# Two groups' second layer in one pass, its first product by Strassen's seven block products

## The chip, the cores and the metric

The kernel runs on one core of a Trainium2 chip. The metric is device time in microseconds (us) of one launch, the median of several runs. Five engines work from queues of their own, each strictly in its order: PE (TensorE, matrix products), DVE (VectorE), ACT (ScalarE), POOL (GpSimd) and SP (SyncE, here only the issuer of transfers).

## The reference

Three stages follow each other on 1152 tokens (batch 2 x 576) of width 512. In short:

```python
# attention, 8 heads of 64, causal, with a bias from cumulated gates
cum = cumsum(maximum(s, 0), axis=-1)
scores = where(causal, -1e9, q @ k.T / 8 + minimum(-(cum[q] - cum[k]), 0))
x = softmax(scores) @ v                      # -> (1152, 512)
# layer 1: 512 -> 2048 -> 512, w_in and w_out
h = x @ w_in
x = where(h > 0, h, exp(minimum(h, 0)) - 1) @ w_out
# layer 2: E = 4 experts, 512 -> 1024 -> 512, weighted by p = probs / sum(probs)
for e in range(4):
    out += p[:, e:e+1] * (maximum(x @ w1[e], 0) @ w2[e])
```

## The kernel before

The tokens are cut into three groups, `GROUPS` = (0, 256), (256, 384), (640, 512) as (first token, tokens). For each group the kernel does attention, then layer 1, then layer 2. A layer's weights are cut into *units* of 128 hidden columns: a unit is one tile [128, 1024], its first half the piece of the first matrix (four blocks of 128 input rows), its second half the piece of the second. Layer 1 has `NAB` = 16 units, layer 2 has `E * NCD` = 4 x 8 = 32.

*Precision.* Except in layer 1 of the first group, an fp32 product is made of three matmuls of rounded operands (`three`, L540): high x high, high x low, low x high. So weights are split once for each group by `prepare` (L77): ACT rounds (L81), DVE takes the remainder (`split_lo`, L64).

*A unit.* `up1` or `up2` makes the hidden values of all the group's tokens, 4 x 3 matmuls with the tokens as columns, into a PSUM bank `up`; ACT and DVE apply the nonlinearity and split the result into `gt`. `LAG` = 2 units later `down1` (12 matmuls into four banks acc0 to acc3, result transposed) or `down2` (3 matmuls of 512 columns for each 128 tokens) adds the unit's share of the second product. In layer 2 the four accumulators run over the 8 units of an expert, then DVE scales them by p and adds them to `osb` (L710, L712); at the last expert the tile goes out (L715). Between the layers the accumulated `yacc` is rounded by ACT and split by DVE into yh and yl (L682).

*Transfers.* Layer 1's weights come coded (`w64`), 32 half units; the decoder borrows free tiles for them, and writes the decoded units to HBM (`w_dec`), from where the later groups load them. `fetch` (L72) loads units into `raw` (three buffers), `prepare` works from there.

*Order.* `slot` (L576) is the loop's step: `up` of a unit, preparation of later units (`advance`), `down` of an earlier one. Attention of the *next* group is cut into small parts (`attention_parts`) that `Background` hands out evenly between `BG_FROM` and `BG_TO`: the middle group's from slot 14 of the first group to its end, the last group's from slot 17 of the middle group (where its layer 2 begins) to its end. A scheduler then fixes each engine's order from this.

Of the kernel before, what the change touches and what calls it, by code (L numbers as in the profile page):

```python
# [25 lines left out]
GROUPS = [(0, 256), (256, 384), (640, 512)]  # L26
CHUNKS = [[0, 128, 256, 384, 512, 576], [0, 64, 192, 320, 448, 576]]
JOBS = [
    [],
    [(0, (2, 3, 4), 0), (1, (0,), 320)],  # L30
    [(1, (1, 2), 0), (1, (3, 4), 256)],
]

# [5 lines left out]
BG_FROM = [14, 17, 0]  # L39
BG_TO = [1, 2, 0]  # L40
# [7 lines left out]
def tile_kernel(ctx, tc, qT, kT, v, s, w64, w, probs, out):  # L48
    nc = tc.nc
    pool = ctx.enter_context(tc.tile_pool(name="sb", bufs=1))  # L50
    psum = ctx.enter_context(tc.tile_pool(name="ps", bufs=1, space=bass.MemoryType.PSUM))
    PE, DVE, ACT, POOL, SP = nc.tensor, nc.vector, nc.scalar, nc.gpsimd, nc.sync

    def sb(shape, tag, bufs, dtype=F32):
        return pool.tile(shape, dtype, tag=tag, name=tag, bufs=bufs)
# [13 lines left out]
    n_units = NU * len(GROUPS)  # L69
    fetched, units = {}, {}  # L70

    def fetch(n):  # L72
        u = n % NU
        fetched[n] = t = sb([128, 1024], "raw", 3)
        SP.dma_start(out=t, in_=w_dec[u] if u < NAB else w[u - NAB])
# [11 lines left out]
    small = [(t, 1, 1) for t in ("yh0", "yl0", "yh1", "yl1")] + [("raw", 3, 1)] * 3 + [("xl", 1, 2)]  # L87
    turn = [("wu", 5, 2)] * N_WU + [("gt", 3, 1)] * N_GT + small * 5
# [24 lines left out]
    def decode_halves(upto):  # L113
# [4 lines left out]
        while n_decoded[0] < min(upto, len(order)):  # L118
# [10 lines left out]
            z = sb([128, 512], f"osb{i % 2}", 1, I32)  # L129
# [198 lines left out]
    def attention_parts(g, xh, xl):  # L328


        items, jobs = [], ([], [])
        for b, chunks, col in JOBS[g]:
            cb = CHUNKS[b]
            q0, q1 = cb[chunks[0]], cb[chunks[-1] + 1]
            for hp in range(HP):
                job = dict(b=b, chunks=chunks, col=col, q0=q0, q1=q1, hp=hp, small=q1 == 64)
# [5 lines left out]
                jobs[job["small"]].append(job)  # L342

        def load_small():

            b = jobs[1][0]["b"]
            q, k, ck, vv = (sb([128, HP, 1, n], t + "s", 1)
                            for t, n in (("q2", 64), ("k2", 64), ("cbp", 64), ("v", 128)))
            for t, x in ((q, qT), (k, kT)):
                SP.dma_start(out=t[:, :, 0], in_=x[b, :, 0:64].rearrange("(c p) n -> p c n", p=128))  # L350
            for j in range(2):
                rows = cum_d[b * H:b * H + H, 0:64].rearrange("(o c j) k -> o j c k", o=1, j=2)
                SP.dma_start(out=ck[64 * j:64 * j + 64, :, 0],
                             in_=rows[:, j].to_broadcast([64, HP, 64]))
            SP.dma_start(out=vv[:64].rearrange("p c o n -> p (c o n)"), in_=v[b, 0:64])
            for job in jobs[1]:
                hp = job["hp"]
                job["q"], job["k"], job["cump"], job["v"] = q[:, hp], k[:, hp], ck[:, hp], vv[:, hp]
                job["pt"] = sb([128, 2, 1, 64], "pts", HP)

        def load(job):
# [30 lines left out]
            job["pt"] = buf([128, 2, nc_, nq], "pt")  # L392
# [22 lines left out]
        def qk(it, pss, a, e):  # L415
# [9 lines left out]
            for jj in range(2):  # L425
                r = slice(64 * jj, 64 * jj + 64)
                x = 0 if job["small"] else jj
                PE.matmul(pss[r, :e - a], job["q"][r, x, qs], job["k"][r, x, a:e],  # L428
# [37 lines left out]
        def transposes(it, cs):  # L466
# [5 lines left out]
            for m, c in enumerate(cs):  # L472
                PE.transpose(pt[:cb[c + 1] - cb[c], m, :], p[:, cb[c]:cb[c + 1]], ident)  # L473
            dst, m0 = job["pt"], 0
# [14 lines left out]
        def values(job):  # L489
# [11 lines left out]
            ACT.activation(xh[:, hp, xs], o[:, :nq], AF.Copy)  # L501
            split_lo(xl[:, hp, xs], o[:, :nq], xh[:, hp, xs])
            big = jobs[0]
            if job in big and big.index(job) + 2 < len(big):
                load(big[big.index(job) + 2])
# [4 lines left out]
        def start():  # L510
            with late():
                for job in jobs[0][:2]:
                    load(job)
                if jobs[1]:
                    load_small()
# [79 lines left out]

    x_first = sb([128, NCC, GROUPS[0][1]], "xh", 1)
    attention_first(x_first)
    cum_columns(0, 4)
    cum_columns(1, 0)
    n_use = 0  # L600
    x_parts = None
    for g, (t0, tok) in enumerate(GROUPS):
        n_tile = tok // 128
# [19 lines left out]
        class Lazy(list):  # L623

            def __init__(self, f, n):
                super().__init__([None] * n)
                self.f, self.got = f, None

            def __getitem__(self, i):
                if self.got is None:  # L630
                    self.got = self.f()
                return self.got[i]

        def up1(n, k, x):
# [141 lines left out]
```

## Time and profile before

| | us |
|---|---|
| median of 3 runs | 737.17 (736.9 to 739.24) |
| the profiled execution | 739.13 |
| its span, first to last instruction | 737.2 |
| PE busy | 707.3 (96%) |
| PE weight loads busy | 601.1 (82%) |
| DVE busy | 450.2 (61%) |
| ACT busy | 384.5 (52%) |

Stages on PE, by the chain: start and attention of the first group to 35.5 us; its layer 1 to 104.6 and layer 2 to 227.3; the middle group's layer 1 to 300.8 and layer 2 to 467.8; the last group's layer 1 to 558.9 and layer 2 to 731.2. A line number stands for a line of the kernel; L544 is the matmul in `three`, so all its products share it, and are told apart by their tiles and columns. Idle time of an engine counts only where it is the one that others wait for.

### The profile page before, as it was taken

The page shows a single profiled execution, that of the slowest core. Times are in us where ns is not written, and L with a number is a line of the kernel's source. Part 1 is how long each engine was busy: PE and PEld are TensorE (multiplying, and loading weights), DVE is VectorE, ACT ScalarE, POOL GpSimd, SP SyncE. Part 2 cuts the span into 40 slices and gives each one's busy share as a digit, 9 for nine tenths or more (in the row PEclk, how much of TensorE's full clock was granted, in tenths as well). Part 3 has the DMA queues.
Part 4 walks back from the last instruction along what each step waited for, and adds up shares of the span by engine and source line. Part 5 has one row for each costly group of instructions (what it writes and reads, how often), then busy time and mean ns, then how long its engine had stood idle before and what let it go on. Part 6 is the DMA issues. An engine that isn't in the chain of part 4 may idle for free.

```text
span 737.2 us, 10366 instructions
## 1 busy us (share of the span) xinstructions
PE 707.3 (96%) x3738; PEld 601.1 (82%) x3738; DVE 450.2 (61%) x899; ACT 384.5 (52%) x766; POOL 13.6 (2%) x33
## 2 busy tenths in 40 slices
PE   5489799999999999999999999999999999999997
PEld 4378678878879999888888888888888888888886
DVE  4678687977766666868777664565554344343432
ACT  4978676866645454766665555444344323332220
POOL 2001000000000000000000000000000000000000
PEclk9599999999999999999999999999999999999999
DMA  9689988755645343455543332333233232332301
GB/s 323 237 300 389 279 281 228 200 186 162 194 147 197 116 130 127 122 175 153 179 135 103 117 102 86 130 120 108 86 106 94 88 112 86 94 106 87 114 1 57
DMA packets 45298, 111.64 MB, mean 151 GB/s; under 512 B 7392, under 2 KB 18528, under 8 KB 45248
## 3 DMA queue, kind: packets, MB, share of 16 engines
q1 hardware_dynamic: 42784, 102.34, 43.7%
q0 software_dynamic: 2304, 8.39, 2.8%
q8 instruction: 29, 0.48, 0.3%
q10 hardware_dynamic: 160, 0.26, 0.1%
q14 instruction: 21, 0.17, 0.1%
HBM read 99.96 MB, written 11.01 MB: 151 GB/s over the span
## 4 chain that ended last, share of the span: by engine, by line
PE 83%; DVE 5%; DMA 5%; ACT 4%; issue 2%; SPq 0%; DVEq 0%; ACTq 0%
PE acc L544 37%; PE up L544 37%; PE att L498 3%; PE att L473 3%; DMA raw<-in_w 1%; ACT wu L128 1%; DVE wu L131 1%; PE att L422 1%; PE att L420 1%; DMA q<-in_qT 1%; ACT osb L130 1%; DMA wu<-in_w 1%; DMA yh<-in_w 1%; PE att L428 1%; PE up L640 1%
## 5 line engine op out<-in xcount | busy, mean ns | idle before, releaser
L544 PE MATMUL acc<-wu,gt 128*128 128x512 f32 x864 | 226.8, 398 | 0.0
L64 DVE TENSOR_TENSOR wu<-raw,wu 128x1024 fp32r<-128x1024 f32 x128 | 156.6, 1223 | 113.5 <-ACT wu L81 113.4
L544 PE MATMUL up<-yh,wu 128*128 128x256 f32 (+2 forms) x768 | 208.4, 340 | 0.0
L81 ACT ACTIVATE wu<-raw 128x1024 fp32r<-128x1024 f32 x128 | 135.5, 1059 | 94.3 <-PE acc L544 92.7
L544 PEld LDWEIGHTS acc<-wu,gt 128*128 128x128 f32 x864 | 155.7, 188 | 30.7 <-issue 3.2
L544 PEld LDWEIGHTS up<-yh,wu 128*128 128x128 f32 x768 | 136.6, 188 | 13.3 <-issue 1.2
L544 PE MATMUL up<-yl,wu 128*128 128x256 f32 (+2 forms) x384 | 129.3, 337 | 0.6 <-DVE yl L64 0.6
L726 ACT ACTIVATE gt<-up 128x256 fp32r<-128x256 f32 (+2 forms) x96 | 46.9, 489 | 93.8 <-PE up L544 93.4
L544 PE MATMUL acc<-gt,wu 128*128 128x384 f32 (+1 forms) x384 | 81.3, 362 | 0.0
L727 DVE SCALAR_TENSOR_TENSOR gt<-up,gt 128x256 fp32r<-128x256 f32 (+2 forms) x96 | 53.2, 554 | 44.5 <-ACT gt L726 44.2
L544 PEld LDWEIGHTS up<-yl,wu 128*128 128x128 f32 x384 | 72.4, 189 | 7.6 <-DVE yl L64 1.7
L544 PE MATMUL up<-xh,wu 128*128 128x384 f32 (+1 forms) x256 | 77.0, 362 | 0.0
L544 PEld LDWEIGHTS acc<-gt,wu 128*128 128x128 f32 x384 | 69.5, 188 | 7.5
L544 PEld LDWEIGHTS up<-xh,wu 128*128 128x128 f32 x256 | 47.4, 188 | 5.1
L644 ACT ACTIVATE e<-up 128x256 f32<-128x256 f32 (+2 forms) x48 | 23.4, 488 | 47.1 <-PE up L544 42.7
L544 PE MATMUL up<-xl,wu 128*128 128x384 f32 (+1 forms) x128 | 46.3, 362 | 0.0
L463 ACT ACTIVATE p<-p,nm 128x576 f32<-128x576 f32 (+6 forms) x56 | 34.5, 616 | 15.5 <-DVE nm L458 15.2
L640 PE MATMUL up<-xh,wu 128*128 128x256 f32 x128 | 32.0, 394 | 6.4 <-DVE gt L648 5.5
L655 ACT ACTIVATE gt<-e 128x384 fp32r<-128x384 f32 (+1 forms) x32 | 18.5, 577 | 32.8 <-DVE e L652 32.8
L458 DVE CUSTOM_DVE_ANT_0 p<-att,mask 128x384 f32<-128x384 f32 (+5 forms) x48 | 25.2, 525 | 15.5 <-PE att L422 15.5
L640 PEld LDWEIGHTS up<-xh,wu 128*128 128x128 f32 x128 | 24.7, 197 | 11.0 <-DVE gt L648 6.7
L473 PE MATMUL att<-ident,p 128*128 128x128 f32 (+1 forms) x192 | 32.1, 273 | 0.6 <-DVE p L438 0.3
(135 smaller groups left out, 673.5 us busy)
## 6 DMA issues: line engine op xcount, KB each, us to landing
raw<-in_w SPq DMA_DIRECT2D x105, 512.0 KB
raw<-w_dec SPq DMA_DIRECT2D x32, 512.0 KB
w_dec<-wu POOLq DMA_DIRECT2D x16, 512.0 KB, 7.0
k<-in_kT SPq DMA_DIRECT2D x16, 288.0 KB
yh<-in_w SPq DMA_DIRECT2D x6, 512.0 KB
yl<-in_w SPq DMA_DIRECT2D x6, 512.0 KB
xl<-in_w SPq DMA_DIRECT2D x6, 512.0 KB
out<-osb SPq DMA_DIRECT2D x9, 256.0 KB
```

Of the source, the lines that this page charges most:

```text
L64: DVE.tensor_tensor(out=lo, in0=x, in1=hi.bitcast(F32), op=ALU.subtract)
L81: ACT.activation(t[:, 0], x, AF.Copy)
L458: DVE.tensor_tensor_reduce(p[:, a:e], pss[:, :e - a], it["bias"][:, a:e], -1.0 / SC, it["low"], ALU.add, ALU.min, nm)
L463: ACT.activation(p, p, AF.Exp, bias=nm, scale=-1.0, accum_out=sm)
L473: PE.transpose(pt[:cb[c + 1] - cb[c], m, :], p[:, cb[c]:cb[c + 1]], ident)
L498: PE.matmul(o[64 * j:64 * j + 64, qs:nq], job["v"][:n, c, 64 * j:64 * j + 64], job["pt"][:n, j, c, qs:nq], start=c == 0, stop=c == n_c - 1)
L544: PE.matmul(o, a[m], b[n], start=first and i == 0, stop=last and i == 2)
L640: PE.matmul(o, t[:, dm(c)], x[:, c], start=c == 0, stop=c == NCC - 1)
L644: ACT.activation(e, o, AF.Exp)
L655: ACT.activation(gt[:, 0], e, AF.Copy)
L726: ACT.activation(ht[:, 0], o, AF.Relu)
L727: DVE.scalar_tensor_tensor(out=ht[:, 1], in0=o, scalar=0.0, in1=ht[:, 0].bitcast(F32), op0=ALU.max, op1=ALU.subtract)
```

## The change

The groups become (0, 256), (256, 448), (704, 448), and both batches cut their rows at 0, 128, 256, 384, 512, 576. The middle group is rows 0 to 127 of batch 1 and 256 to 575 of batch 0. The first group stays as it was but for its buffers. Then comes layer 1 of the middle group, with the last group's attention in its background (`BG_FROM[1]` = 0), then layer 1 of the last group, then one layer 2 for both.

Layer 2 takes two units (a *pair*, 256 hidden columns) at a time. The inputs are the blocks A11, A12 (middle group, first and second half of the 512 inputs) and A21, A22 (last group); the weights of a pair are B11, B21 (first unit) and B12, B22. With sums S1 to S4 of the A (made once, on DVE) and T1 to T4 of the B (for each pair, on DVE, `sums`), seven block products give the four blocks of hidden values, for two units and both groups; each is 2 x 3 matmuls of 448 columns (`up_mm`) where eight would do it directly. Two of the seven accumulate on another's bank (p2 on p1's, p4 on p7's, p3 on p5's), the others are added by DVE (`add`). The second product is `down`: for each of the seven 128-token tiles six matmuls of 512 columns for a pair, after which DVE adds the scaled result to `ox` (before: once in 8 units). Weights of layer 2 for these groups are loaded and split once, by pair, into two buffers `raw2`. The first two pairs are prepared in layer 1 of the last group (`hook` takes one step of `early` per slot).

```diff
-GROUPS = [(0, 256), (256, 384), (640, 512)]
-CHUNKS = [[0, 128, 256, 384, 512, 576], [0, 64, 192, 320, 448, 576]]
+GROUPS = [(0, 256), (256, 448), (704, 448)]
+CHUNKS = [[0, 128, 256, 384, 512, 576]] * B
...
-BG_FROM = [14, 17, 0]
-BG_TO = [1, 2, 0]
+BG_FROM = [14, 0, 0]
+BG_TO = [1, 1, 0]
...
-    small = [(t, 1, 1) for t in ("yh0", "yl0", "yh1", "yl1")] + [("raw", 3, 1)] * 3 + [("xl", 1, 2)]
+    small = [("yh", 1, 1), ("yl", 1, 1)] + [("raw", 3, 1)] * 3 + [("xa", 1, 3), ("ox", 1, 3)]
...
+            DVE.tensor_tensor(out=t[:, 0], in0=b12, in1=b11, op=ALU.subtract)
+            DVE.tensor_tensor(out=t[:, 1], in0=b22, in1=b12, op=ALU.subtract)
+            DVE.tensor_tensor(out=t[:, 2], in0=b22, in1=t[:, 0], op=ALU.subtract)
+            DVE.tensor_tensor(out=t[:, 3], in0=b21, in1=t[:, 2], op=ALU.subtract)
...
+        def low_2():
+            split_lo(w2s[q][:, 1], raws[q][:, :, 512:1024], w2s[q][:, 0])
+            if q + 2 < n_pair:
+                load_pair(q + 2)
...
+        return [high, low, sums, high_t, low_t, high_2, low_2]
...
+    early = [first_blocks(0), first_blocks(1)] + pair_steps(0) + pair_steps(1)
...
+    yacc = layer1(2, xs[2], lambda at: None, hook)
...
+    def up_mm(q, bank, block, op, first, last):
+        x = blocks[block]
+        for c in range(2):
+            cs = slice(128 * c, 128 * c + 128)
+            for i, (m, n) in enumerate(((0, 0), (0, 1), (1, 0))):
+                PE.matmul(bank, tops[q][:, m, op, cs], x[:, n, c], start=first and c + i == 0,
+                          stop=c == 1 and i == 2, skip_group_check=True)
...
+        up_mm(q, st["a"], "A11", B11, True, True)
+        st["p1"] = tmp("p1")
+        ACT.activation(st["p1"], st["a"], AF.Copy)
...
+        up_mm(q, st["a"], "A12", B21, False, True)
+        relu(q, 0, 0, st["a"])
...
+        up_mm(q, b, "S2", T2_, True, True)
+        st["u2"] = add("u2", b, st["p1"])
...
+    split("A22", A22)
...
+    DVE.tensor_tensor(out=s12, in0=A21, in1=A22, op=ALU.add)
+    split("S1", s12)
+    DVE.tensor_tensor(out=s12, in0=s12, in1=A11, op=ALU.subtract)
+    split("S2", s12)
+    DVE.tensor_tensor(out=s34, in0=A11, in1=A21, op=ALU.subtract)
+    split("S3", s34)
+    DVE.tensor_tensor(out=s12, in0=A12, in1=s12, op=ALU.subtract)
+    split("S4", s12)
...
+    for q in range(1, n_pair):
+        ups = [(p6,), (p7,), (p5, c22), (p4, c21), (p3,)]
+        if q > 1:
+            ups = [(p1,), (p6,), (p2,)] + ups[1:]
+        steps = pair_steps(q + 1) if q + 1 < n_pair else []
+        for i in range(NCH):
+            for f in ups.pop(0) if ups else ():
+                f(q)
+            down(q - 1, i)()
+            if steps:
+                steps.pop(0)()
```

PE where the last group's attention runs. Before, in layer 2 of the middle group (yh: its input, att: attention's banks, 384 columns for the group's tokens):

```order
L544 MATMUL acc0_3730<-wu_3481,gt_3588 128x512 x3
L544 MATMUL acc1_3731<-wu_3481,gt_3588 128x512 x3
L420 MATMUL att_3750<-kh_3611,qs_3610 128x320
L422 MATMUL att_3750<-kl_3613,qb_3612 128x320
L544 MATMUL acc2_3732<-wu_3481,gt_3588 128x512 x3
L473 MATMUL att_3764<-ident_64,p_3624 64x128
L473 MATMUL att_3764<-ident_64,p_3624 128x128 x2
L544 MATMUL up_3770<-yh0_3037,wu_3659 128x384
L544 MATMUL up_3770<-yl0_3038,wu_3659 128x384
L544 MATMUL up_3770<-yh0_3037,wu_3659 128x384 x2
```

After, in layer 1 of the middle group (xa: its input; lines moved by the edit, L558 is `three`):

```order
L434 MATMUL att_3244<-kh_3181,qs_3180 128x512
L436 MATMUL att_3244<-kl_3183,qb_3182 128x512
L486 MATMUL att_3255<-ident_70,p_3156 128x128 x2
L558 MATMUL acc0_2736<-gt_3058,wu_2894 128x448 x3
L558 MATMUL acc1_2737<-gt_3058,wu_2894 128x448 x3
L434 MATMUL att_3270<-kh_3234,qs_3233 128x512
L436 MATMUL att_3270<-kl_3236,qb_3235 128x512
L558 MATMUL acc2_2738<-gt_3058,wu_2894 128x448 x3
L558 MATMUL acc3_2739<-gt_3058,wu_2894 128x448 x3
L486 MATMUL att_3287<-ident_70,p_3194 128x128 x3
L513 MATMUL att_3292<-pt_3178,v_2951 64x256
L558 MATMUL up_3313<-xa_783,wu_3163 128x448 x4
```

The attention matmuls stand between those of a unit of layer 1 now, two row blocks to a unit.

PE at the entry into layer 2. Before, from layer 1 (acc from gt) to layer 2 (up from yh and yl) of the last group:

```order
L544 MATMUL acc2_5044<-gt_5519,wu_5450 128x512 x3
L544 MATMUL acc3_5045<-gt_5519,wu_5450 128x512 x3
L544 MATMUL up_5586<-yh0_5563,wu_5487 128x512
L544 MATMUL up_5607<-yh0_5563,wu_5524 128x512
L544 MATMUL up_5586<-yl0_5564,wu_5487 128x512
L544 MATMUL up_5586<-yh0_5563,wu_5487 128x512 x2
L544 MATMUL up_5586<-yl0_5564,wu_5487 128x512
L544 MATMUL up_5586<-yh0_5563,wu_5487 128x512
L544 MATMUL up_5586<-yh1_5569,wu_5487 128x512
L544 MATMUL up_5586<-yl1_5570,wu_5487 128x512
```

After, from layer 1 of the last group to the first two pairs (x2a: A11 and A12; A22, S1 to S4: the blocks made at this point; top: the pair's weights; w2, h: the second product):

```order
L558 MATMUL acc2_4067<-gt_4571,wu_4496 128x448 x3
L558 MATMUL acc3_4068<-gt_4571,wu_4496 128x448 x3
L878 MATMUL up_4622<-x2a_3985,top_4159 128x448 x6
L878 MATMUL up_4640<-x2a_3985,top_4435 128x448 x5
L878 MATMUL up_4622<-x2a_3985,top_4159 128x448 x6
L878 MATMUL up_4640<-x2a_3985,top_4435 128x448
L878 MATMUL acc0_4683<-A22_4661,top_4159 128x448 x5
L878 MATMUL up_4640<-x2a_3985,top_4435 128x448 x6
L878 MATMUL acc0_4683<-A22_4661,top_4159 128x448
L878 MATMUL att_4690<-S1_4667,top_4159 128x448 x6
L878 MATMUL att_4706<-S3_4675,top_4159 128x448
L558 MATMUL acc1_4763<-w2_4160,h_4621 128x512
```

Twenty-four matmuls on A11 and A12 are placed first, with five of the first block product on A22 among them; the order takes the others up one by one.

DVE in layer 2. Before, two units at an expert's end (wu: weight split, gt: hidden values, osb: the scaled sums):

```order
L64 TENSOR_TENSOR wu_6153<-raw_6085,wu_6153 128x1024
L727 SCALAR_TENSOR_TENSOR gt_6148<-up_6135,gt_6148 128x512
L712 SCALAR_TENSOR_TENSOR osb0_5582<-acc0_5921,pr_5575,osb0_5582 128x512
L712 SCALAR_TENSOR_TENSOR osb1_5583<-acc1_5922,pr_5575,osb1_5583 128x512
L712 SCALAR_TENSOR_TENSOR osb2_5584<-acc2_5923,pr_5575,osb2_5584 128x512
L712 SCALAR_TENSOR_TENSOR osb3_5585<-acc3_5924,pr_5575,osb3_5585 128x512
L64 TENSOR_TENSOR wu_6190<-raw_6118,wu_6190 128x1024
L727 SCALAR_TENSOR_TENSOR gt_6185<-up_6172,gt_6185 128x512
```

After, about half a pair in the middle of the loop (raw2: the loaded pair, top and w2: its weights' remainders, ox: the scaled sums, u2, c: sums of block products):

```order
L79 TENSOR_TENSOR top_5713<-raw2_5553,top_5713 128x512
L79 TENSOR_TENSOR top_5713<-raw2_5553,top_5713 128x256
L889 SCALAR_TENSOR_TENSOR h_5555<-c_5680,h_5555 128x448
L626 SCALAR_TENSOR_TENSOR ox_4682<-acc2_5684,pr_4614,ox_4682 128x512
L79 TENSOR_TENSOR top_5713<-sums_5752,top_5713 128x1024
L79 TENSOR_TENSOR w2_5574<-raw2_5413,w2_5574 128x1024
L626 SCALAR_TENSOR_TENSOR ox_4682<-acc0_5705,pr_4614,ox_4682 128x512
L894 TENSOR_TENSOR u2_5724<-up_5717,p1_5703 128x448
L626 SCALAR_TENSOR_TENSOR ox_4682<-acc1_5726,pr_4614,ox_4682 128x512
L889 SCALAR_TENSOR_TENSOR h_5695<-up_5696,h_5695 128x448
L626 SCALAR_TENSOR_TENSOR ox_4682<-acc2_5744,pr_4614,ox_4682 128x512
L804 TENSOR_TENSOR sums_5892<-raw2_5693 128x256
```

The buffer that w2's remainder reads last, `raw2_5413`, is the one that `raw2_5693` is loaded into, and five instructions stand between it and the first sum of that pair; the scaled sums (L626), which stood at an expert's end, now stand in every pair.

## Rows read from the trace of the kernel before

**Rows 1.** The page: span, busy time of PE, its granted clock in 40 slices.
```profile
span 737.2 us, 10366 instructions
...
PE 707.3 (96%) x3738; PEld 601.1 (82%) x3738; DVE 450.2 (61%) x899; ACT 384.5 (52%) x766; POOL 13.6 (2%) x33
...
PEclk9599999999999999999999999999999999999999
```

**Rows 2.** Waits of PE: engine line, waited for, us in total, times, longest.
```profile
PE att L294 <- DVE k L287: 7.0, 1, 7.0
PE acc L259 <- DMA pt<-in_kT: 6.8, 1, 6.8
...
PE up L544 <- DVE yl L64: 0.6, 2, 0.4
```

**Rows 3.** Stretches: us, busy and count by engine, clock, DMA share, GB/s.
```profile
35.50:104.60 69.10, 62.69 (x294) 53.32 (x293) 52.95 (x112) 52.50 (x111) 7.44 (x14) 0.97 0.92 314
104.60:227.30 122.70, 122.26 (x810) 99.15 (x809) 90.69 (x214) 79.83 (x175) 0.00 (x0) 1.00 0.63 187
300.80:467.80 167.00, 166.94 (x955) 143.26 (x956) 114.64 (x275) 98.54 (x240) 0.00 (x0) 1.00 0.42 128
...
130.00:150.00 20.00, 20.00 (x131) 16.28 (x131) 18.80 (x43) 15.56 (x33) 0.00 (x0) 1.00 0.72 213
80.00:90.00 10.00, 6.02 (x22) 4.68 (x21) 5.02 (x8) 6.44 (x15) 0.53 (x1) 0.85 0.88 280
```

**Rows 4.** The chain that ended last: start us, us, what.
```profile
77.55 10.23 DMA raw<-in_w
...
273.82 2.08 PE acc L544 x12
...
637.95 2.72 PE acc L544 x12
```

**Rows 5.** DVE's groups by form: count, busy us, mean ns, idle before.
```profile
L64 DVE TENSOR_TENSOR wu<-raw,wu 128x1024 fp32r<-128x1024 f32 x128 | 156.6, 1223 | 113.5 <-ACT wu L81 113.4
...
L727 DVE SCALAR_TENSOR_TENSOR gt<-up,gt 128x512 fp32r<-128x512 f32 x32 | 22.1, 692 | 41.7 <-ACT gt L726 41.7
...
L712 DVE SCALAR_TENSOR_TENSOR osb<-acc,pr,osb 128x512 f32<-128x512 f32 x27 | 19.1, 745 | 5.0 <-PE acc L544 5.0
...
L727 DVE SCALAR_TENSOR_TENSOR gt<-up,gt 128x384 fp32r<-128x384 f32 x32 | 17.7, 553 | 2.2 <-ACT gt L726 2.1
...
L64 DVE TENSOR_TENSOR gt<-e,gt 128x512 fp32r<-128x512 f32 x16 | 11.1, 692 | 10.5 <-ACT gt L655 10.5
...
L651 DVE TENSOR_SCALAR e<-e 128x512 f32<-128x512 f32 x16 | 6.8, 428 | 15.9 <-ACT e L644 15.9
L64 DVE TENSOR_TENSOR qs<-q,qs 64x256 fp32r<-64x256 f32 x16 | 6.8, 423 | 0.5
...
L710 DVE TENSOR_SCALAR osb<-acc,pr 128x512 f32<-128x512 f32 x9 | 6.3, 743 | 0.1
```

**Rows 6.** Timeline of DVE from 598 us: start us, us, what.
```profile
606.59 2.72 DVE L710 TENSOR_SCALAR osb<-acc,pr 128x512 f32<-128x512 f32 x4
609.22 1.22 DVE L64 TENSOR_TENSOR wu<-raw,wu 128x1024 fp32r<-128x1024 f32 x1
```

**Rows 7.** Timeline of SP's queue at 605 us: a unit's load is issued.
```profile
604.98 0.34 SPq L75 DMA_DIRECT2D raw<-in_w  x1
```

**Rows 8.** Half microseconds after it; the last number is GB/s moved.
```profile
605.50:606.00 0.50, 0.50 (x4) 0.42 (x3) 0.02 (x1) 0.45 (x1) 0.00 (x0) 1.00 0.22 49
...
607.00:607.50 0.50, 0.50 (x4) 0.42 (x3) 0.50 (x2) 0.00 (x0) 0.00 (x0) 1.00 0.85 344
...
608.00:608.50 0.50, 0.50 (x4) 0.42 (x3) 0.50 (x1) 0.43 (x1) 0.00 (x0) 1.00 0.19 74
```

**Rows 9.** Waits of DVE: the round trip through ACT in layer 1.
```profile
DVE gt L64 <- ACT gt L655: 18.8, 29, 0.8
```

**Rows 10.** Timeline of the tail, DVE and SP's queue, from 729 us.
```profile
731.15 2.79 DVE L712 SCALAR_TENSOR_TENSOR osb<-acc,pr,osb 128x512 f32<-128x512 f32 x4 [4.80 <-PE acc L544]
...
731.93 2.37 SPq L715 DMA_DIRECT2D out<-osb  x4
```

More of the change, by code (lines that the diff above doesn't have):

```diff
@@ L733, in tile_kernel @@
[L733 to L738 removed]
+        for k in range(NAB + LAG):
+            slot(n_use[0], k, up1(n_use[0], k) if k < NAB else None, background)
+            hook(k)
+            if k < NAB:
+                n_use[0] += 1
+        return [yacc[c][:, :tok] for c in range(NCC)]
+    x_first = sb([128, NCC, GROUPS[0][1]], "xf", 1)
@@ new lines, in up2, with f @@
+    def up2(n, m):
+        def f():
+            t = units[n]
+            o = ps("up", 2)[:, :tok]
+            for c in range(NCC):
+                three(o, halves(t, 0, dm(c)), (yh[:, c], yl[:, c]), c == 0, c == NCC - 1)
+            ht = sb([128, 2, tok], "gt", 3, F32R)
+            ACT.activation(ht[:, 0], o, AF.Relu)
+            DVE.scalar_tensor_tensor(out=ht[:, 1], in0=o, scalar=0.0, in1=ht[:, 0].bitcast(F32),
+                                     op0=ALU.max, op1=ALU.subtract)
+            pend.append(Lazy(lambda: down2(t, ht, m // NCD, m % NCD), n_tile))
+        return f
@@ new lines, in tile_kernel, with keep @@
+    for m in range(E * NCD):
+        slot(n_use[0], NAB + LAG + m, up2(n_use[0], m), background)
+        n_use[0] += 1
+    assert background.got.done == len(background.got.parts)
+    xs[2] = sb([128, 2, NCC, N2], "ox", 1, F32R)
+    background = Background(attention_parts(2, xs[2]), BG_FROM[1], NAB + LAG - BG_TO[1])
+    yacc = layer1(1, xs[1], background)
+    assert background.done == len(background.parts)
+    y = sb([128, NCC, 2 * N2], "xa", 1)
+    def keep(c, half):
+        o = y[:, c, N2 * half:N2 * half + N2]
+        if c % 2:
+            DVE.tensor_copy(o, yacc[c])
+        else:
+            ACT.activation(o, yacc[c], AF.Copy)
@@ new lines, in c22, with p4, c21, p3 @@
+    def c22(q):
+        st = state[q]
+        relu(q, 1, 1, add("c", st["e"], st["u3"]))
+    def p4(q, own=None):
+        st = state[q]
+        o, u = (st["c"], "u2") if own is None else (bank(own), "u3")
+        st["p4"] = o
+        up_mm(q, o, "A22", T4, own is not None, True)
+        st["c21"] = u
+    def c21(q):
+        st = state[q]
+        relu(q, 0, 1, add("c", st["p4"], st[st["c21"]]))
+    def p3(q):
+        st = state[q]
+        up_mm(q, st["e"], "S4", B22, False, True)
+        relu(q, 1, 0, add("c", st["e"], st["u2"]))
@@ L742 @@
+    for i in range(NCH):
+        down(n_pair - 1, i)()
 def kernel(**inputs):
```

353 lines of the change are left out of this document (230 added, 123 removed).

## The prediction

> **What bounds the kernel now.** I read four views in this order. First the page's totals: PE is busy for 707.3 of 737.2 us, and its granted clock is full in almost every slice after the start [rows 1]. Then PE's waits: what it lacks is 29.9 us, nearly all of it single waits of several us in the first 90 us; after that there are only waits of tenths [rows 2]. Third, the busy time by stage: from 104.6 us to the end PE is full, while DVE is at 74% beside the first group's layer 2 (90.69 of 122.70 us) and at 69% beside the middle group's (114.64 of 167.00), where the attention of the next group runs too [rows 3]. Last, the chain: in the layers it is nothing but PE, in blocks of equal price [rows 4]. So PE's own work is the bound; a matmul that is taken away is worth its pace, as long as DVE, ACT and the loads still hide behind what is left.
>
> Twelve matmuls of 384 columns take 2.08 us in the chain and twelve of 512 take 2.72 [rows 4], so 173.3 and 226.7 ns each: 0.417 ns a column (a column per tick of 2.4 GHz) and 13.3 ns beside it. A matmul of 448 columns, which the trace does not show, lies in the middle of the two: 200 ns.
>
> **The change, part by part.**
>
> *1. Matmuls.* Layer 1 of the two later groups has 16 units x 24 matmuls for each group: before at 384 and at 512 columns, 384 x (173.3 + 226.7 ns) = 153.6 us; after 768 x 200 ns = 153.6 us. The regrouping alone changes nothing. Layer 2's second product is 32 units x 21 matmuls of 512 columns before and 16 pairs x 42 after, the same. Layer 2's first product was 32 x 12 matmuls for each group, 768 in all, 384 x (173.3 + 226.7) = 153.6 us; now it is 16 pairs x 7 blocks x 6 matmuls of 448 columns, 672 x 200 ns = 134.4 us. Gone: 96 matmuls, **-19.2 us**. Priced at the two neighbours it would be 16.6 to 21.8.
>
> *2. Attention's cut.* Batch 1's blocks now begin at multiples of 128. By the order of the instructions the last group's attention falls from 67,584 to 62,976 columns, and the middle group's rises from 55,296 to 57,856. In the stages that hold them attention takes PE what the layer's matmuls leave: 167.0 - 32 x (2.08 + 9 x 0.2267) = 35.1 us, and 122.7 - 32 x (12 x 0.120 + 6 x 0.2267) = 33.1 us [rows 3, 4] (0.120 for 256 columns by the same line). So -2.4 and +1.5: **-0.9 us** (-3 to +2).
>
> *3. The last group's attention moves from layer 2 of the middle group into its layer 1.* That is the risk of the middle of the program. PE's work there is 16 x 24 x 0.2 = 76.8 us and 35.1 - 2.4 = 32.7 of attention: 109.5 us. DVE: of 114.64 us in the old stage, 32 weight splits and 32 splits of 384 columns take 32 x (1.223 + 0.553) = 56.8, nine evictions 6.7 [rows 3, 5], so attention cost 51; seven row blocks per head pair instead of eight make it about 50. A unit of layer 1 costs a weight split 1.22, a clamp 0.39 (0.43 at 512 columns), and two ops of 448 columns at 0.62, between the rows of 384 and 512: 2.86 us, 46 for 16 [rows 5]. Sum 96 of 109.5 us, 88%. From 130 to 150 us DVE was at 18.80 of 20.00 us with PE at 20.00 [rows 3], so 88% need not cost anything; the whole-stage share that was seen with PE full is only 74%, and if DVE could not pass that, the stage would last 96/0.74 = 130 us, 20 more. The value is near the first row: **+4 us** (0 to 20). DVE's lag would show as PE waiting for p and gt.
>
> *4. The start of the last group's layer 1.* ACT has the first pair's weights to round (they come by a load that can start only when attention's tiles are free) queued ahead of the second unit's exp. A load ahead of ACT's queue is what cost 10.23 us on the chain at 77.55, when the DMA engines were at 88% [rows 3, 4]; here they are under half loaded. **+1 us** (0 to 10).
>
> *5. Entry into layer 2.* Before, the group's result was rounded and the next matmuls followed at once. Now four sums and five splits of 896 columns stand in a row on DVE, about 9 x 1.09 = 9.8 us (on the line from 0.692 at 512 to 1.223 at 1024 columns [rows 5]), and the evictions. PE has, in the order that the program was given, 24 matmuls of the first two pairs (4.8 us) that need none of this, then p4, p5, p7, p6, p3 as each operand comes, with second-product matmuls in between: 110 matmuls, 22.6 us of work. Going through the two queues by hand, each operand is there within about a microsecond of its turn. **+2 us** (0 to 8; the upper end adds a fall of the clock: in the 10 us with 4 us of idle it was granted 0.85, between its levels of 1.2 and 2.4 GHz [rows 3]).
>
> *6. The loop over pairs.* PE has 42 x 0.2 + 42 x 0.2267 = 17.92 us a pair. DVE's work for a pair is, at the durations of [rows 5], 7 evictions of 0.745, 9 ops of 448 at 0.62, four sums of 256 columns at 0.42 (the row of that width), and the remainders of the rounding in pieces of 512, 256, 1024 and 1024: 0.69 + 0.42 + 2 x 1.22; together 16.0 us, 90% of PE's. The loop is closer still: the pair buffer is freed by w2's remainder; then the load must land, the sums, evictions, three chains through ACT and the remainders follow in DVE's queue, until w2's remainder comes again. A load of 512 KB was issued at 604.98 and its last bytes moved before 608.5 [rows 7, 8]; a pair has twice that, at the 344 GB/s of the middle another 1.5 us: 4.9 us. The 19 DVE ops add up to 12.5 us at full durations, and two round trips to ACT at 0.65 (18.8 us over 29 waits [rows 9]) 1.3: 18.7 us, more than PE's 17.92. But four evictions of 0.743 started 0.657 apart (2.63 us to the next op's start) [rows 5, 6]: some 0.08 us less for each of 16 that follow without a wait, so 17.4 us. PE stays the bound by half a microsecond. **+2 us** for the 12 pairs that load (0 to 33, with the dearest reading of both terms).
>
> The Trainium skill, on the page "VectorE: DVE Perf Modes", section "The DRAIN you can't avoid", says that the next op does not start until the pipe has emptied, and to lower the number of ops; read strictly, the loop is 18.7 us. The 0.657 us above speaks against that reading, in this trace.
>
> *7. First group, decoder and tail.* 16 half units of the first weights can be on their way instead of 14, and the `raw` buffers hold the last of them, so the first layer-2 load starts a slot later: **0** (-4 to +4, the 4 us of idle between 80 and 90 [rows 3]). The tail keeps its form, one last eviction and the way out of its tile [rows 10]: 0. The 32 fewer unit loads cost nothing before, PE did not wait for them.
>
> Sum: -19.2 - 0.9 + 4 + 1 + 2 + 2 = -11.1. The profiled execution took 739.13 us (737.2 of span and 1.9 around it), so 728.0; that execution lies 2.0 above the median of the runs, 737.17, so **726 us** for the median.
>
> **Rivals.**
>
> *A: everything hides* (items 3 to 6 at 0). The trace speaks for it with the 20 us at 94% of DVE, against it stand new queues with 90% everywhere: 737.2 - 20.1 = 717 us. Chance 0.16.
>
> *B: DVE's queue in the strict form* in the loop, as by the rule named above: 18.7 - 17.9 = 0.8 us x 12 pairs = 10, in place of 2: 734 us. The overlap in [rows 6] speaks against it. Chance 0.10.
>
> *C: the attention stage is held at DVE's old share* (+20 in place of 4): 742 us. For it: three engines at 75 to 100% that answer each other, against it 130 to 150 us. Chance 0.12.
>
> *D, slower:* the loop over pairs is bound by load and DVE, at the place where the sums wait for the pair's weights with u3 and an eviction queued behind. If the pair's load takes twice the 3.4 us of a single one, 6.8, and ops take their full time, the period is 20.6 us, 2.7 x 12 = 32 us more: 756 us. It decides from a period of 19.2 us (then it eats what else is won). For it: the sums come only 5 us of PE time after the load's release; against it: the load runs at 344 GB/s with the engines idle around it. Chance 0.06.
>
> *E: the change does not do what it says* (the block products need more matmuls, or their sums stand on PE): the order has exactly 672 matmuls of 448 columns; 737 us, chance 0.01.
>
> My forecast's own case, a net gain of 6 to 16 us, has 0.55; its own range is 721 to 731. About 0.3% (2.2 us) is what can be told from no change. Faster: the forecast's case, A and half of B, 0.76; the same: the other half of B, a quarter of C and E, 0.09; slower: the rest of C, and D, 0.15. The range, 715 to 741, takes in A, B and a part of C.
>
> **What would show it.** Right: layer 2 of the pairs runs at 17.9 us a pair in the chain, PE only; the stage of layer 1 with attention lasts 110 to 114 us; PE's waits after 110 us stay under 10 us. Item 6 is wrong if DVE's sums wait for the raw pair and PE for h; item 3 if PE waits for p, gt or the probabilities for more than 8 us; item 5 if the first p4 to p3 lie over more than 26 us; item 1 if a matmul of 448 columns is not 200 ns apart.

## The result, and the profile after

The changed kernel takes 730.45 us, the median of four runs (728.78 to 733.32), beside 738.2 for the kernel before (four runs, measured with it): 7.8 us less, a ratio of 0.9896, 95% interval 0.985 to 0.9941. Its profiled execution took 728.78 us with a span of 726.9, 10.3 less than before. That execution is the fastest of its four, while the profiled one of the kernel before (739.13) lay above its median, so some 2.5 us of the 10.3 are spread between executions; what follows compares these two traces.

The page of the changed kernel, for [rows 1]:

```profile
span 726.9 us, 10237 instructions
...
PE 696.2 (96%) x3626; PEld 591.2 (81%) x3626; DVE 560.1 (77%) x1142; ACT 371.2 (51%) x777; POOL 13.6 (2%) x33
...
PEclk9599999999999999999999999999999999999999
```

The waits of PE in the changed kernel, for [rows 2]:

```profile
PE att L308 <- DVE k L301: 7.5, 1, 7.5
PE acc L273 <- DMA pt<-in_kT: 6.8, 1, 6.8
...
PE up L558 <- DVE yl L79: 1.0, 1, 1.0
...
PE up L558 <- DVE e L684: 0.6, 1, 0.6
```

Stretches of the changed kernel, columns as in [rows 3]: the middle group's layer 1 with the last group's attention; the last group's layer 1; the pairs, and a piece of them for later:

```profile
228.60:348.90 120.30, 120.12 (x698) 99.18 (x697) 98.27 (x257) 83.93 (x198) 0.00 (x0) 1.00 0.44 132
...
348.90:428.20 79.30, 78.66 (x386) 72.18 (x385) 53.14 (x84) 38.25 (x57) 0.00 (x0) 1.00 0.32 116
428.20:723.00 294.80, 294.80 (x1344) 251.70 (x1342) 237.04 (x373) 86.18 (x141) 0.00 (x0) 1.00 0.13 48
...
480.00:700.00 220.00, 220.00 (x1006) 188.52 (x1005) 175.32 (x281) 63.73 (x105) 0.00 (x0) 1.00 0.15 52
```

The chain of the changed kernel, for [rows 4]: layer 1 of the last group, one pair from its first `acc` to the next pair's, the last second products:

```profile
364.65 2.46 PE up L558 x12
367.12 2.42 PE acc L558 x12
...
464.71 1.40 PE acc L558 x6
466.11 1.23 PE att L878 x6
...
483.11 1.40 PE acc L558 x6
...
711.81 11.26 PE acc L558 x48
```

PE waits even less than forecast: in the 374 us of the last two stretches it lacks 0.6 us, and DVE, at 82% beside the attention and 80% in the pairs, holds up next to nothing. But a matmul is slower than forecast. Six of 512 columns take 1.40 us, 233 ns each where [rows 4] gave 226.7; six of 448 take 1.23, 205 ns where I had put 200. A pair takes 483.11 - 464.71 = 18.40 us, not 17.92. Even the last 48, all of 512 columns, stay at 11.26/48 = 234.6 ns.

Adding up, in either trace, the time from each matmul's start to the next one's from the first group's layer 2 on (104.6 and 105.0 us) gives, in us:

| | before | changed |
|---|---|---|
| first products of the later groups | 234.5 (1152 matmuls) | 219.3 (1056) |
| second products of 384 to 512 columns (with 192 of the first group) | 282.6 (1247) | 286.5 (1247) |
| the first group's 256 columns | 47.9 | 47.2 |
| attention of the later groups | 63.1 | 64.6 |
| sum | 628.2 | 617.6 |

The rest is 0.4 us more at the start and 0.2 less at the tail. The first products give back 15.2 us for 96 matmuls fewer, the second products, the same in number, take 3.9 more. So what wanted testing was the pace.

The kernel before, too, has matmuls of 512 columns that are slower than in [rows 4]. In its middle group's layer 2, where they stand between blocks of 384 columns and attention's matmuls, its chain shows six in a row at 232 ns each:

```profile
381.93 1.39 PE acc L544 x6
```

### The profile page after: what moved, and what is told of

It is laid out like the page before. It is cut to its first block, busy times and chain, and to the rows that moved or that the text cites. A ratio compares the mean times of both kernels' runs of the same rounds, so it can differ in the third digit from the quotient of the medians.

```text
span 726.9 us, 10237 instructions
## 1 busy us (share of the span) xinstructions
PE 696.2 (96%) x3626; PEld 591.2 (81%) x3626; DVE 560.1 (77%) x1142; ACT 371.2 (51%) x777; POOL 13.6 (2%) x33
## 4 chain that ended last, share of the span: by engine, by line
PE 86%; DMA 6%; ACT 3%; DVE 2%; issue 1%; SPq 1%; DVEq 0%; ACTq 0%
PE acc L558 39%; PE up L558 16%; PE att L878 11%; PE up L878 8%; PE att L513 3%; PE att L486 3%; DMA cbp<-cum_d 2%; DMA pt<-in_kT 2%; PE up L672 2%; PE acc L659 2%; PE att L441 1%; PE att L434 1%; PE att L436 1%; DMA wu<-in_w 1%; DMA raw<-in_w 1%
## 5 line engine op out<-in xcount | busy, mean ns | idle before, releaser
L558 PE MATMUL acc<-w,h 128*128 128x512 f32 x672 | 174.4, 396 | 0.0
L558 PEld LDWEIGHTS acc<-w,h 128*128 128x128 f32 x672 | 126.1, 188 | 25.1 <-ACT h L888 0.2
L79 DVE TENSOR_TENSOR wu<-raw,wu 128x1024 fp32r<-128x1024 f32 x64 | 78.2, 1222 | 21.2 <-ACT wu L95 20.4
L626 DVE SCALAR_TENSOR_TENSOR ox<-acc,pr,ox 128x512 f32<-128x512 f32 x105 | 78.5, 748 | 13.0 <-PE acc L558 10.4
L558 PE MATMUL acc<-gt,wu 128*128 128x448 f32 x384 | 87.8, 371 | 0.0
L95 ACT ACTIVATE wu<-raw 128x1024 fp32r<-128x1024 f32 x64 | 67.5, 1054 | 20.5 <-PE acc L558 15.3
L558 PEld LDWEIGHTS acc<-gt,wu 128*128 128x128 f32 x384 | 70.1, 188 | 7.9 <-issue 2.6
L878 PE MATMUL att<-S,top 128*128 128x448 f32 x288 | 67.2, 368 | 0.0
L878 PEld LDWEIGHTS att<-S,top 128*128 128x128 f32 x288 | 54.0, 188 | 7.8 <-issue 0.2
L558 PE MATMUL acc<-wu,gt 128*128 128x512 f32 x192 | 56.4, 409 | 0.0
L558 PE MATMUL up<-yh,wu 128*128 128x256 f32 x256 | 52.6, 287 | 0.0
L558 PEld LDWEIGHTS up<-yh,wu 128*128 128x128 f32 x256 | 41.9, 190 | 2.7 <-issue 1.7
L558 PE MATMUL up<-xa,wu 128*128 128x448 f32 x192 | 43.8, 372 | 0.0
L558 PE MATMUL up<-ox,wu 128*128 128x448 f32 x192 | 42.0, 368 | 0.6 <-DVE e L684 0.6
L476 ACT ACTIVATE p<-p,nm 128x384 f32<-128x384 f32 (+4 forms) x56 | 34.5, 616 | 13.6 <-DVE nm L471 13.3
L676 ACT ACTIVATE e<-up 128x448 f32<-128x448 f32 (+1 forms) x48 | 23.4, 488 | 33.3 <-PE up L558 31.4
L558 PEld LDWEIGHTS up<-ox,wu 128*128 128x128 f32 x192 | 36.0, 188 | 4.2 <-DVE e L684 1.0
```

The source lines that it names most:

```text
L79: DVE.tensor_tensor(out=lo, in0=x, in1=hi.bitcast(F32), op=ALU.subtract)
L95: ACT.activation(t[:, 0], x, AF.Copy)
L476: ACT.activation(p, p, AF.Exp, bias=nm, scale=-1.0, accum_out=sm)
L558: PE.matmul(o, a[m], b[n], start=first and i == 0, stop=last and i == 2)
L626: DVE.scalar_tensor_tensor(out=o_sb, in0=o, scalar=pr[:, i, e:e + 1], in1=o_sb, op0=ALU.mult, op1=ALU.add)
L676: ACT.activation(e, o, AF.Exp)
```

## The experiments

In the built program one can read where each tile begins in a partition. Before, both operands of every matmul of the layers begin 64 bytes beyond a multiple of 512. In the changed kernel, which puts its pools at both ends of the memory, w2 and top begin at remainder 384, h at 480, the S blocks and A22 at 480 or 224, A11 and A12 at 384 or 128, wu at 480, gt at 480 or 224, layer 1's inputs at 64 or 320; and a row of 448 columns is 3.5 x 512 bytes.

**All tiles at multiples of 64 bytes (e1_aligned)**

```diff
+    edge = ctx.enter_context(tc.tile_pool(name="edge", bufs=1, side="right"))
+    nc.gpsimd.memset(edge.tile([128, 8], F32, tag="edge", name="edge", bufs=1), 0.0)
```

> The changed kernel with one idle tile of 32 bytes a partition put at the far end of SBUF, so that every tile of the two right-hand pools (weights, gt, yh, yl, h, A22, S1 to S4) begins 32 bytes lower, at a multiple of 64 bytes, as all of them did in the kernel before. Nothing else moves. Theory T1 (place in memory): a matmul of the loop lasts 233.5 instead of 226.7 ns at 512 columns and 204.6 instead of 200 at 448 because operands begin 32 bytes beside a multiple of 64. Then 512 columns come back to 226.7 and 448 to 200, the pair from 18.40 to 17.92 us, layer 1 from 4.88 to 4.80 us a unit, and the time from 730 to 719 to 721. Rival T2 (columns): blocks of 448 columns, or the change between 448 and 512, are slower in themselves; the pair stays at 18.40 us, 730. Rival T3 (contention): a DVE at 80% disturbs PE's reads or writes; the pair stays at 18.40 us, 730.

Measured 729.17 us, ratio to before 0.9873 (0.9846 to 0.9901). Its chain:

```profile
642.58 1.40 PE acc L558 x6
643.98 1.22 PE up L878 x6
...
713.22 11.21 PE acc L558 x48
```

The pace hardly moves (the last 48 at 233.5 ns). T1 falls in this form. Note for later that w2 and h are still unequal, 64 bytes apart in place of 96.

**The kernel before, all tiles 32 bytes on (e2_before_off)**

```diff
+    edge = ctx.enter_context(tc.tile_pool(name="edge", bufs=1))
+    nc.gpsimd.memset(edge.tile([128, 8], F32, tag="edge", name="edge", bufs=1), 0.0)
     pool = ctx.enter_context(tc.tile_pool(name="sb", bufs=1))
```

> The kernel before with an idle tile of 32 bytes ahead of its only pool, so that all operands begin 32 bytes beside a multiple of 64. T1: the pure 512-column stretch after 468 us, where matmuls start 226.7 ns apart, goes to about 234 ns as in the changed kernel's tail; some 1600 matmuls of 512 columns at +7 ns give +11 us, those of 384 columns 0 to +4: 746 to 753. T2 and T3: nothing changes, 737 to 738.

Measured 738.79 us, ratio 0.9996 (0.9977 to 1.0016). Its chain has twelve matmuls of 512 columns at 2.72 us, as in [rows 4]:

```profile
721.48 2.72 PE up L546 x12
```

The place itself does not count: T1 falls a second time.

**Eight direct products in place of seven (e3_direct)**

```diff
-    B11, B21, B22, T1, T3, T2_, T4 = range(7)
...
+    for q in range(1, n_pair):
+        ups = [(f,) for f in second]
+        if q > 1:
+            ups = [(first[0], first[1])] + [(f,) for f in first[2:] + second]
```

> The changed kernel with the seven block products undone: one pass over pairs for both groups as before it, but the first product as four direct products of 12 matmuls of 448 columns (48 a pair in place of 42), without the sums of weights, the sums of inputs and the five additions. 96 more matmuls of 448 columns. T1 and T2: at the pace of the changed kernel's loop, 204.6 ns, +19.6 us: 750, with 19.6 us a pair. T3: DVE has about 5 us less work a pair, and the pace goes back to 200 and 226.7 ns: 19.1 us a pair, 742.

Measured 749.74 us, ratio 1.0145 (1.0116 to 1.0175). Its chain shows 19.57 us a pair:

```profile
616.77 2.43 PE up L848 x12
636.34 2.43 PE up L848 x12
```

19.3 us more than the changed kernel by the medians (18.4 by the two ratios to the kernel before), as T1 and T2 had it: 96 matmuls at some 200 ns. DVE has much less to do than in the changed kernel, and the pace is the same, so T3 misses:

```profile
480.00:700.00 220.00, 220.00 (x1014) 190.05 (x1013) 114.30 (x148) 46.51 (x68) 0.00 (x0) 1.00 0.16 53
```

And it is 10.8 us *slower* than before: one pass over regrouped tokens, in this layout and without the block products, loses.

**Narrow evictions (e4_narrow_evict)**

```diff
-            evict(o_all[:, i], o, pr, i, q * 2 // NCD, q == 0, q == n_pair - 1, T2)
+            evict(o_all[:, i, 0:64] if 0 < q < n_pair - 1 else o_all[:, i], o[:, 0:64] ...)
```

> The changed kernel with the evictions of pairs 1 to 14 narrowed to 64 of 512 columns (the other 448 columns of their sums are left out), so DVE's work in the loop falls from 14.7 us a pair to about 11, with PE's instructions the same. T3: the pair goes from 18.40 toward 17.92 us (18.0 to 18.2), the time to 724 to 727. T1 and T2: 18.40 us a pair, 730.

Measured 730.59 us (one run). The stretch of the pairs, PE, PEld, DVE, ACT:

```profile
480.00:700.00 220.00, 220.00 (x1006) 188.57 (x1005) 139.26 (x280) 63.66 (x105) 0.00 (x0) 1.00 0.15 52
```

The changed kernel has 175.32 us of DVE there, and the same 1006 matmuls recorded. A fifth of DVE's work gone changes nothing in the pace: T3 falls.

**One remainder for both operands (e5_all512)**

```diff
-        blocks[name] = t = l2b.tile([128, 2, 2, N2], F32R, tag=name, name=name, bufs=1)
+        blocks[name] = t = l2b.tile([128, 2, 2, 512], F32R, tag=name, name=name, bufs=1)[:, :, :, :N2]
...
-    xa = l2a.tile([128, 2, NCC, N2], F32R, tag="x2a", name="x2a", bufs=1)
+    xa = l2a.tile([128, 2, NCC, 512], F32R, tag="x2a", name="x2a", bufs=1)[:, :, :, :N2]
```

with idle tiles of 448, 192 and 480 bytes ahead of three pools, and the same 512 for the last group's inputs and for gt.

> The changed kernel with its tiles placed so that both operands of every matmul of the last group's layer 1 and of the pairs begin at the same remainder to 512 bytes: gaps ahead of the pools, and the rows of 448 columns (inputs of the last group, gt, A, S blocks) laid out 512 columns apart. The middle group's inputs keep rows of 448 columns (two of its four chunks lie 256 bytes off). Theory T4 (relative place): it is the difference of the two operands' places that counts, as in the kernel before, where all of them had one remainder, and not the place itself. Then 512 columns go to 226.7 ns and 448 to 200: the pair from 18.40 to 17.92 us unless DVE's queue binds, layer 1 of the last group from 4.88 to 4.80 us a unit; 719 to 722. Rival T6 (form): the pace hangs on how many matmuls go to one bank or on 448 columns; the pace stays as in the changed kernel, 729 to 731.

Measured 726.86 us, ratio 0.9837 (0.981 to 0.9864). Its chain: layer 1, `acc` one pair apart with a block of 448 columns between, the last 48:

```profile
369.49 2.48 PE up L559 x12
371.96 2.48 PE acc L559 x12
...
605.28 1.38 PE acc L559 x6
606.66 1.21 PE up L880 x6
...
623.43 1.38 PE acc L559 x6
...
709.01 10.91 PE acc L559 x48
```

Half of T4 comes out. 512 columns alone run at 10.91/48 = 227.3 ns again, and a pair falls to 18.15 us. But in it the first matmuls of 512 columns after a block of 448 still start 236, 228, 232, 231 and 227 ns apart, and 448 columns stay above 200: 1.21/6 = 202 ns in the pairs, and in layer 1, where nothing else runs, 2.48/12 = 206.7 ns. There they are *slower* than in the changed kernel, whose second products (gt and wu, 0 or 256 bytes apart) took 2.42/12 = 202 and whose first (inputs and wu, 96 or 352 apart) 2.46/12 = 205. So at 448 columns the distance does not order the pace, and T4 fails for them.

**The kernel before with operands 64 bytes, and 256 bytes, apart (e6_before_gap64, e7_before_gap256)**

```diff
             tag, bufs, many, k = places[i]
+            if tag == "gt" and not gap:
+                gap.append(sb([128, 16], "gap", 1))        # e7: 64 columns
+                POOL.memset(gap[0], 0.0)
```

> The kernel before with an idle tile of 64 bytes between the weight tiles (wu) and the tiles behind them (gt, yh0 to yl1), so that the two operands of a matmul begin 64 bytes apart to 512. T4: in the stretch of 512 columns alone after 468 us matmuls start 232 to 234 ns apart instead of 226.7, and 384 columns above 173; some 1600 of the one at +6.5 ns and the other's 0 to +4 us: 747 to 753. T6: nothing changes, 737 to 739.

> The same with 256 bytes between them, the distance that a row of 448 columns puts between two chunks of an input. T4 with a grain of 512 bytes: the same 747 to 753; with a grain of 256 bytes or less: 737 to 739. T6: 737 to 739.

64 bytes: 744.93 us, ratio 1.0084 (1.0055 to 1.0112). 256 bytes: 739.16 (one run, before 738.43). The chain of the first, in layer 1 of the middle group (384 columns) and of the last (512), then in the last group's layer 2:

```profile
255.76 2.09 PE acc L548 x12
...
503.79 2.77 PE up L548 x12
506.56 2.76 PE acc L548 x12
...
718.12 2.80 PE acc L548 x12
720.92 2.79 PE up L548 x12
```

and of the second:

```profile
719.29 2.72 PE acc L548 x12
722.01 2.72 PE up L548 x12
```

So at 512 columns the distance between the operands' places counts: 64 bytes cost 5 to 7 ns a matmul in layer 2 and 3 to 4 in layer 1, 256 nothing, and shifting both together (e2) nothing. Matmuls of 384 columns hardly feel it: 2.09 us for twelve, 2.08 in [rows 4]. That is why the price, 6.5 us, is below the 9 to 15 expected. T6 falls as the only cause; that 448 columns and the changes of column count have a share of their own stays open after e5.

**How near DVE and the loads are to binding in the pairs (e8_narrow_up, e12_320)**

```diff
-                PE.matmul(bank, tops[q][:, m, op, cs], x[:, n, c], start=first and c + i == 0,
-                          stop=c == 1 and i == 2, skip_group_check=True)
+                k = N2 if c + i == 0 else 256        # e12: 320
+                PE.matmul(bank[:, :k], tops[q][:, m, op, cs], x[:, n, c, :k],
+                          start=first and c + i == 0, stop=c == 1 and i == 2, skip_group_check=True)
```

> The changed kernel with five of the six matmuls of every block product in the pairs narrowed from 448 to 256 columns (that part of the first product is left out), so that PE has about 15.4 us of work a pair (7 x (0.203 + 5 x 0.120) + 42 x 0.233) while loads, DVE and ACT have what they had. The period then shows what the loop over load and DVE needs by itself. Forecast of item 6 (DVE's ops overlap by 0.08 us): 17.4 us a pair, PE waiting some 2 us in each for sums' weights or for h. Rival B (no overlap): 18.7, which would show as a period above the 18.40 of the changed kernel. If nothing but DVE's own time counted: 14.7, and PE stays the bound at 15.4.

> The changed kernel with five of the six matmuls of every block product in the pairs narrowed from 448 to 320 columns (that part of the first product is left out): about 16.4 us of PE's work a pair (7 x (0.203 + 5 x 0.147) + 42 x 0.233). DVE's order keeps the form that the forecast walked through, the remainder of w2, the load into the pair buffer that it frees, the next sums from that buffer; narrowed to 256 columns the order had been another, with eight ops between the load's start and the first sum. Forecast of item 6: the loop over load and DVE needs 17.4 us, so PE waits 1.0 us a pair behind the sums. As read from the changed kernel (5.0 us from the end of w2's remainder to the sums, then 13.4 to the end of the next remainder): 18.4, so PE waits 2 us a pair. If the loop gives way, because its ACT waits shrink: 16.4 and no wait.

Measured 689.69 and 704.72 us (one run each). A stretch and two blocks of e8, a pair apart:

```profile
500.00:640.00 140.00, 140.00 (x760) 120.17 (x759) 130.43 (x218) 51.04 (x82) 0.00 (x0) 1.00 0.19 68
```

```profile
536.35 1.64 PE acc L558 x7
...
551.90 1.63 PE acc L558 x7
```

The same of e12 (two blocks, then a stretch); then a block of one matmul of 448 and five of 320 columns and the next matmul, from its PE timeline; then two rows of its DVE timeline, the remainder of w2 that frees a pair buffer and the first sum that needs the load into it:

```profile
526.89 1.64 PE acc L558 x7
...
543.38 1.64 PE acc L558 x7
```

```profile
500.00:660.00 160.00, 160.00 (x816) 139.25 (x815) 142.27 (x234) 53.79 (x89) 0.00 (x0) 1.00 0.17 60
```

```profile
535.37 1.10 PE L879 MATMUL att<-A,top 128*128 128x448 f32 x6
536.31 0.40 PE L558 MATMUL acc<-w,h 128*128 128x512 f32 x1
```

```profile
526.43 1.22 DVE L79 TENSOR_TENSOR w<-raw,w 128x1024 fp32r<-128x1024 f32 x1
...
532.55 0.43 DVE L804 TENSOR_TENSOR sums<-raw 128x256 f32<-128x256 f32 x1
```

15.55 and 16.49 us a pair, PE full in both, with DVE at 130.43/140 = 93% in the first. The loop over load and DVE needs no more than 16.5 us. The load is as forecast (from 527.65 to 532.55, 4.9 us); what gives way is the rest, 13.4 us from the first sum to the end of the next remainder in the changed kernel, 11.6 here: the work of DVE in it is the same, so its waits for ACT and PE were slack.

Ahead of the loop, where the S blocks are made, PE waits in both, in e8:

```profile
PE att L879 <- DVE u L895: 2.4, 1, 2.4
PE up L879 <- ACT S L973: 0.9, 1, 0.9
```

**The attention stage with less of PE's work (e9_narrow_l1)**

```diff
-            PE.matmul(o, a[m], b[n], start=first and i == 0, stop=last and i == 2)
+            r, to = (b[n][:, 0:k], o[:, 0:k]) if i and k < 512 else (b[n], o)
+            PE.matmul(to, a[m], r, start=first and i == 0, stop=last and i == 2)
```

(k is 256 in the middle group's layer 1.)

> The changed kernel with two of three matmuls of the middle group's layer 1 narrowed from 448 to 256 columns (that part of the products is left out): PE's work in the stage with the last group's attention falls by 256 x 0.084 = 21 us, from 121.2 to about 100, while DVE keeps its 99.0 us. Forecast of item 3 (DVE can go to 94% beside a full PE): the stage shrinks from 121.4 to about 106 us, and PE waits for p, gt or probabilities some 6 us. Rival C (held at a share of DVE near what was seen, 74 to 82%): the stage stays at 120 us or more, and PE waits for 20.

Measured 710.84 us (one run). The stage, from its first to the next layer's first matmul:

```profile
229.20:326.10 96.90, 96.17 (x673) 81.61 (x672) 90.36 (x253) 79.64 (x191) 0.00 (x0) 1.00 0.53 161
```

It shrinks by 23.4 us, to DVE at 93% with PE at 99%. Behind it PE waits 2.5 us once for e:

```profile
PE up L558 <- DVE e L685: 2.5, 1, 2.5
```

The bound near 94% stands and rival C falls, but the stage is 9 us shorter than the 106 forecast. The forecast took DVE's busy time, about 99 us, for its work; pressed, 253 instructions cover 90.4 us where 257 covered 98.3. Their durations add up to 106.9 and 109.7 us, so what shrank is not the work: instructions that follow without a wait overlap, as in [rows 6].

**Equal remainders in the pairs alone, and blocks issued two by two (e10_pairs512, e11_doubled)**

Both have e5's gaps and rows for the pairs; the cut shows what e11 adds.

```diff
+            for fs in ups[i:i + 2]:
+                for f in fs:
+                    f(q)
+            for j in range(i, min(i + 2, NCH)):
+                down(q - 1, j)()
```

> The changed kernel with the gaps and the 512-column rows for the pairs alone; layer 1 keeps the places of the changed kernel, where a matmul of 448 columns took 203.5 ns, while with one remainder for both operands it took 206.7 in the last group's layer 1. Theory T4 with that second finding: pairs at 18.15 us, layer 1 of the last group at 4.88 us a unit and not 4.96: 725 to 726. Rival: a pair's pace depends on something else that the other placing changed; 730.

> The same, and in the loop two blocks of the first product are issued in a row and then two of the second, so that only half as many changes between 448 and 512 columns are left (7 or 8 a pair in place of 14). If a matmul of 512 columns after one of 448 is slow for the first five or so (236, 228, 232, 231, 227 ns, then 226.7), each change that goes gives back 21 ns: 0.07 us a pair, 724 to 725. If DVE suffers from two evictions that come together, PE waits for h and it is 726 or more.

Measured 727.86 us, ratio 0.9861 (0.9845 to 0.9878), and 725.38, ratio 0.9824 (0.9806 to 0.9842). Chain of e10:

```profile
369.52 2.43 PE acc L559 x12
371.96 2.48 PE up L559 x12
...
607.13 1.38 PE acc L559 x6
...
625.28 1.38 PE acc L559 x6
```

Chain of e11, blocks of 12 of 512 columns a pair apart:

```profile
632.89 2.73 PE acc L559 x12
...
650.99 2.73 PE acc L559 x12
```

e10 keeps the 18.15 us of e5. Its layer 1 gets only half of the hoped return (4.91 us a unit, expected 4.88). It did not keep all its places: the gap of 448 bytes ahead of the first pool also moves layer 1's inputs, from remainder 64 to 0 and from 320 to 256, and it is the products of these that got slower (2.48 us for twelve, 2.46 in the changed kernel). The profiled execution came to its first layer 1 of 448 columns at 230.9 us where e5's came at 228.5, a spread that nothing after it explains; the two cannot be told apart by their times. e11 has 18.10 us a pair with some 40% of the changes gone, not half (98 left of 169 between 480 and 700 us); it waits for nothing in the loop, and is the fastest version: 5 us below the changed kernel.

## Why the prediction came out, step by step

The sum was right (-11.1 forecast, -10.3 in the spans), but terms in it were wrong in opposite directions: the matmuls gave 8 us less than forecast, and of the 9 us of waits less than 1 came. That these two nearly cancel is luck; the mechanism, that PE's own work is the bound and 96 matmuls fewer are the gain, held. By the medians the change is 7.8 us, not 11: the forecast of 726 took off 2 us because the profiled execution of the kernel before lay above its median, while that of the changed kernel lies 1.7 below its own.

*Item 1 failed, by the test that the prediction set*: "A matmul of 448 columns, which the trace does not show, lies in the middle of the two: 200 ns", and with it "The regrouping alone changes nothing". At the forecast's prices the first two rows of the table would be 230.4 + 272.4 = 502.8 us before and 211.2 + 272.4 = 483.6 after, -19.2; by the table they were 517.1 and 505.8, -11.3. The kernel before was already 14 us above its own two prices, nearly all of it in the two stages with attention, where its matmuls are not at the pace of [rows 4] (232 ns in the line above, with equal remainders; which neighbour makes them so, no run separates); the changed one is above them everywhere: 448 columns at 205 ns in the pairs and (2.46 + 2.42)/24 = 203 in layer 1, 512 columns beside them at 233. The seven products are worth their 96 matmuls (e3: 19.3 us); the regrouping around them, with its layout, costs 10.8 against the kernel before. In the pairs, where the forecast's 16 x 17.92 = 286.7 us became 294.7 to the last matmul, the operands' places make 4 us (e5: 290.7), the 40% of the changes between 448 and 512 columns that e11 removes 1 us (289.8), and 3 us stay with 448 columns and the changes left. Why 448 columns are dear is not settled: in layer 1 equal remainders made them dearer.

*Item 2* was forecast at -0.9 us and came to +1.5, within its bounds but with the other sign. By the same count the middle group's attention takes 2.8 us more and the last group's 1.3 less, where the columns gave 1.5 more and 2.4 less: its time did not follow the columns alone.

*Items 3 to 6, 9 us of waits, came to under 1 us.* Item 3: the stage lasts 120.3 us, not 110 to 114, but PE idles for 0.2 us of it. The length was mis-reckoned, not a wait. By the count of the table the 384 matmuls of layer 1 take 83.4 us in the stage (217 ns each beside the attention, where the forecast had 200 and 76.8 us), attention 33.8 (forecast 32.7), and 3.2 go to twelve second products of the first group that `LAG` leaves over, which I had not put into it. So the larger part is item 1's pace again. Of the two bounds for DVE the one near 94% was right: e9 goes to 93% with PE at 99%, and PE waits 2.5 us only behind the stage. Item 4: 0.6 us, for e. Item 5: nothing, the 24 early matmuls were cover enough, though not by much: where e8 and e12 narrow them with the others, PE waits 3.3 and 2.6 us there. Item 6: the walk through DVE's queue took its waits for ACT and PE as fixed, though they shrink when PE presses; e12 has the loop at 16.5 us or less, so with 17.92 of PE it would not have been half a microsecond from binding, but 1.4 or more. Rivals B and D are excluded by the period of 18.40 with PE never idle, and by e12; C by e9; E by the table's 1056 first products, 672 of them in the pairs; A had the waits right and the matmuls wrong.

*Item 7*: start and tail moved by 0.4 and -0.2 us; 0 was right.

Together: -11.3 of products, -0.7 in the first group's, +1.5 of attention, +0.4 and -0.2: -10.3.

## What to carry to other kernels

A matmul's price holds for the shape *and the layout* in which it was read: price a new column count from the nearest rows, and from the stage that it will run in (the kernel before already had 512 columns at 232 ns between other widths), keep a few per cent for pace, and after a re-tiling look at where each pair of operands begins. Where PE is full, 93% of DVE is no bound as such; a wait counts only if the queue behind it has no slack. And undo the algorithmic part alone (e3): that tells the gain of the scheme from the price of the regrouping it needs.

## What the hardware showed that I had not expected

- The pace of these fp32 matmuls at 512 columns follows the distance between the places of the two operands: where 512 columns follow 512, 226.7 ns with 0 or 256 bytes between them (to 512), 230 to 234 with 64 (e6, and w2 and h in e1), 234.6 with 96 (w2 and h in the changed kernel); other distances were not tried at this width. Matmuls of 384 columns took 174 ns in place of 173 with 64 bytes. The Trainium skill, page "SBUF — State Buffer", section "Operand start alignment", asks of an fp32 operand only that it begin at a multiple of 4 bytes, and says that this is about legality, not speed; every placement here is legal in that sense, and e6 shows what one of them costs.
- 448 columns do not lie on the line through the others: 202 to 207 ns in the layers wherever they ran in blocks, and the distance does not order them, while 320 columns in e12 take (0.94 - 0.205)/5 = 0.147 us, which is on that line (133.3 + 13.3 ns). Why, no run here tells.
- With equal remainders matmuls of 512 columns are slow for the first four after a block of 448 (e5) and then settle at 226.7; with w2 and h 96 bytes apart they do not settle within 48.
